# Reordering the ramp of a fused chunk-selecting attention and softplus MLP kernel: weights between the first blocks, later blocks loaded as fp32 and cast on GpSimd, first query tile unselected

## The chip, the cores and the metric

The kernel runs on one core of a Trainium2 chip. The metric is device time in microseconds for one launch; the profile beside it is one profiled execution, read engine by engine (PE is TensorE, DVE is VectorE, ACT is ScalarE, POOL is GpSimd, SP is SyncE, which here only issues DMAs).

## What is computed

```python
# attention: q, k, v are (4, 8, 768, 64) fp32; chunks of 32 keys, the best 6 are kept
k_min, k_max = min/max of k over each chunk
ub = sum(maximum(q * k_min, q * k_max), axis=-1)       # upper bound of a chunk
ub = where(causal, ub, -1e9)
top_chunks = argsort(ub)[..., -6:]
scores = where(selected chunk and key <= query, scale * q @ k.T, -1e9)
attn_out = softmax(scores) @ v
# MLP on x = attn_out as (3072, 512):
h = x @ w_in                                           # w_in (512, 2048)
g = maximum(h, 0) + log1p(exp(-abs(h)))                # softplus
out = g @ w_out                                        # w_out (2048, 512)
```

Among queries 0 to 127 of a batch only four chunks are causal at all, fewer than the six that may be kept.

## The kernel before, in words

The work is cut into 12 blocks (`blocks`, 4 batches of 3) of 256 queries. A block n passes through `loads` or the ramp's loads, `prep`, four `attend` steps (one for each pair of heads), `mlp_h` (64 matmuls of 256 columns on `w_in`, then exp and ln on ACT) and `mlp_y` (32 matmuls of 512 columns on `w_out`).

`prep` transposes k and q, takes each chunk's minimum and maximum (DVE, `kx`), multiplies them with the positive and the negative part of q (PE, L458 and L459), finds the sixth largest with MAX8 (L470), writes a 0/1 row for each chunk into `mr` (L476), transposes `mr` and copies it behind q in the tiles `qab`, so that the score matmul adds the mask by itself. The first three blocks (NRAMP, "the ramp") load fp32 on SP's and ACT's queues into eight buffers `xf` and transpose on PE; the other nine load with a cast to bf16 on POOL's queue (L340, L342) and transpose by DMA (L391, L436, L504, L609).

Every operation is a `Task` with an engine, a duration and a priority. `Graph.schedule` plays the program with these numbers and emits the tasks in the order in which it started them; each engine then runs its own list in that order. `after=` holds a task back in this plan only. On the chip an instruction waits for the buffers and tiles that it touches and, if it issues a DMA, for the DMA eight before it on the same kind of queue, and for nothing else. So a late instruction holds everything behind it on its engine, wherever the plan had put it.

Before the change the plan puts the four `w_in` and `w_out` groups (twelve DMAs on POOL's queue, L311 and L317) behind the attention of the first two blocks and in front of the causal masks of the third, which POOL makes as well (L562, one for each head pair's half). `when_att` and `when_mlp` are the priorities; MSTART is the time at which the MLP's begin.

Of the kernel before, what the change touches and what calls it, by code (L numbers as in the profile page):

```python
# [32 lines left out]
NRAMP = 3  # L33


LAT = {"PE": 0.23, "ACT": 0.20, "DVE": 0.15, "POOL": 0.15, "SP": 0.0}
PSUM_CAP = {"s": 3, "h": 3, "y": 2, "o": 2, "t": 3}
# [7 lines left out]
class Task:  # L45
    __slots__ = ("n", "eng", "dur", "lat", "fn", "prio", "deps", "users", "bufs", "wait",
                 "ready", "start", "end", "dma", "name", "order")


class Graph:  # L50
# [6 lines left out]
    def add(self, eng, dur, fn, prio, r=(), w=(), dma=None, lat=None, name="", after=()):  # L57
        t = Task()
        t.n, t.eng, t.dur, t.fn, t.prio, t.dma, t.name = len(self.tasks), eng, dur, fn, prio, dma, name
        t.lat = LAT[eng] if lat is None else lat  # L60
        deps, bufs = set(after), []
# [22 lines left out]
    def schedule(self):  # L84
# [36 lines left out]
        def flow(to):  # L121
            nonlocal moved
            while moved < to:
                live = [q for q in queues.values() if q]
                if not live:
                    moved = to
                    return
                step = min(min(q[0][0] for q in live) * len(live), to - moved)
                moved += step
                for q in live:  # L130
                    q[0][0] -= step / len(live)
# [8 lines left out]
        while True:  # L140
            nxt = events[0][0] if events else None
            live = [q for q in queues.values() if q]
            if live:
                cand = moved + min(q[0][0] for q in live) * len(live)
# [6 lines left out]
            while events and events[0][0] <= now + 1e-9:  # L151
# [10 lines left out]
                elif what == "queue":  # L162
                    queues.setdefault(x.eng, []).append([x.dma, x])
            for e in LAT:
# [26 lines left out]
                else:  # L191
                    post(now + 1.1, "queue", t)
# [4 lines left out]
def build(nc, tiles):  # L197
# [20 lines left out]
    MSTART = 28.0  # L218
# [3 lines left out]
    ahead = 1.16  # L222
# [43 lines left out]
    for i in range(2):  # L266
# [6 lines left out]
        def oh(which, i):  # L273
            dst = T("ka", i)[64:96] if which == "ka" else T("kb", i)[32:64]
            src = T("ohb").rearrange("c (j s) -> c j s", s=128).unsqueeze(2)
            PO.tensor_copy(dst, src.to_broadcast([32, NQT, NP, 128]))
        for which in ("ka", "kb"):
            add("POOL", 2.7, lambda which=which, i=i: oh(which, i), -6 + i * 34, r=["ohb"], w=[(which + "c", i)],
                name="oh" + which)
# [14 lines left out]
    for n in range(NRAMP):  # L294
        for nm in "kqv":
            for t in range(NT):
                b_ = XF[nm, n, t] = Buf("xf")
                eng = "ACT" if n == 0 and t == 1 else "SP"
                dur = 0.6

                def ld(nm=nm, n=n, t=t, b_=b_, eng=eng):
                    (AC if eng == "ACT" else SP).dma_start(
                        out=T(b_).rearrange("s (h d) -> s h d", h=H), in_=rows(nm, n, t))
                add(eng, dur, ld, -100 + n * 10 + "kqv".index(nm), w=[b_], dma=1.17, lat=0.5, name=f"ld{nm}{n}{t}")

    gate = []


    def ld_win(half, kt):
        fs = slice(half * DFF // 2, (half + 1) * DFF // 2)  # L310
        PO.dma_start(out=T("w_in")[:, kt, fs], in_=moe_w_in()[kt * 128:(kt + 1) * 128, fs])  # L311

    def moe_w_in():
        return srcs["w_in"]

    def ld_wout(c4):
        PO.dma_start(out=T("w_out")[:, c4 * 4:(c4 + 1) * 4, :],  # L317
                     in_=srcs["w_out"][c4 * 512:(c4 + 1) * 512, :].rearrange("(kt ki) f -> ki kt f", ki=128))

    WGATE = []  # L320

    def weights():
        for half in range(2):
            for kt in range(KDM):
                add("POOL", 0.55, lambda half=half, kt=kt: ld_win(half, kt), 14 + half * 2 + kt * 0.1,
                    w=[("w_in", half, kt)], dma=1.38, lat=0.7, name="ldw_in", after=WGATE)
        for c4 in range(4):
            add("POOL", 0.75, lambda c4=c4: ld_wout(c4), 20 + c4, w=[("w_out", c4)], dma=3.1, lat=0.7, name="ldw_out",
                after=WGATE)

    def loads(n):
        base = when_att[n, 0] - 30
        for i, nm in enumerate("kqv"):
# [3 lines left out]
            for t in range(NT):  # L337
                def ld(nm=nm, n=n, t=t, b_=b_):
                    if nm == "v":
                        PO.dma_start(out=v_dst(n, t), in_=rows(nm, n, t))  # L340
                    else:
                        PO.dma_start(out=T(b_)[:, t].rearrange("s (h d) -> s h d", h=H), in_=rows(nm, n, t))  # L342
                b, blk = blocks[n]
                w = [("v", b % 2, blk * NT + t)] if nm == "v" else [(b_, t)]
                add("POOL", 0.9, ld, max(base, 24 + n) + i, w=w, dma=2.1, lat=0.7, name=f"ld{nm}{n}")
# [4 lines left out]
    def prep(n):  # L350
# [9 lines left out]
        ub_sb, mr = Buf("ub"), Buf("mr")  # L360
        if ramp:
            for t in range(NT):
                j = blk * NT + t
                xk = XF["k", n, t]
                kT = ps("t")

                def tr(xk=xk, kT=kT):
                    for p in range(NP):
                        PE.transpose(T(kT)[:, p * 128:(p + 1) * 128], T(xk)[:, p * 128:(p + 1) * 128], T("identf"))
                add("PE", 0.44, tr, pr, r=[xk, "identf"], w=[kT], name=f"kT{n}")  # L370

                def ka(kT=kT, j=j):
                    AC.copy(T("ka", i)[0:64, j], T(kT)[0:64].rearrange("d (p s) -> d p s", p=NP))

                def kb(kT=kT, j=j):
                    AC.copy(T("kb", i)[64:128, j], T(kT)[64:128].rearrange("d (p s) -> d p s", p=NP))

                def red(m, kT=kT, t=t):
# [393 lines left out]
```

## Time and profile before

| | |
|---|---|
| median of 3 runs | 299.5 us (298.94 to 299.71) |
| profiled execution | 298.97 us, of which the span is 297.3 us |
| busy: PE, ACT, DVE, POOL | 252.8, 198.4, 151.6, 113.5 us |
| mean granted clock of TensorE | 0.948 of full speed |

A span is cut by instructions: what an engine waits for is named at the end of its row, and the wait is time before that row's start. Where PE is busy without a gap, only less work for it can shorten the time; where it has gaps, the releaser named is what to follow.

### The profile page before, as it was taken

The numbers are of one execution on the slowest core, as the hardware profiler recorded it, in microseconds if no ns is written. First come the engines' busy times: TensorE is split into PE (matmuls) and PEld (weight loads), VectorE is DVE, ScalarE is ACT, GpSimd is POOL, SyncE is SP. The second block draws the span as 40 slices with busy tenths as digits, with TensorE's granted clock in tenths as the row PEclk, the third lists the DMA queues.
The fourth block names the chain that finished last, engine by engine and source line by source line (L and its number), as shares of the span: only waits on it lengthen the run. The fifth ranks groups of instructions, "written<-read, shape, count | busy, mean of one in ns | idle before, by whom it ended". The sixth has DMA issues, their size and how long they took to land.

```text
span 297.3 us, 6510 instructions
## 1 busy us (share of the span) xinstructions
PE 252.8 (85%) x2465; PEld 188.0 (63%) x2496; DVE 151.6 (51%) x553; ACT 198.4 (67%) x355; POOL 113.5 (38%) x184
## 2 busy tenths in 40 slices
PE   2637652705999999999999999999999999999994
PEld 2416541504896776678766677786867867767661
DVE  5899999631641235376237864175897411010001
ACT  2435760523689674889957398994878968949470
POOL 8956896535591132034654251243312211110000
PEclk9999995565699999999999999999999999999999
DMA  8995999999997158999999984699544211020001
GB/s 162 217 217 113 107 144 153 183 196 173 111 109 72 66 60 125 128 121 90 71 144 173 119 135 54 109 134 113 143 92 56 73 35 72 4 71 37 35 35 71
DMA packets 119647, 32.14 MB, mean 108 GB/s; under 512 B 113472, under 2 KB 115520, under 8 KB 119616
## 3 DMA queue, kind: packets, MB, share of 16 engines
q0 software_dynamic: 59424, 11.28, 47.7%
q1 hardware_dynamic: 57072, 19.67, 35.5%
q10 hardware_dynamic: 3120, 0.79, 1.5%
q8 instruction: 19, 0.31, 0.5%
q14 instruction: 12, 0.10, 0.1%
HBM read 27.26 MB, written 6.29 MB: 113 GB/s over the span
## 4 chain that ended last, share of the span: by engine, by line
PE 69%; DMA 12%; DVE 11%; issue 2%; POOL 2%; ACT 1%; SPq 1%; DVEq 0%; ACTq 0%
PE ps L629 27%; PE ps L651 25%; DMA w_out_sb<-in_moe_w_out_dram 6%; PE ps L542 6%; PE ps L572 6%; DMA w_in_sb<-in_moe_w_in_dram 3%; PE ps L547 3%; DVE kx L379 2%; DMA qab<-kq 2%; PE ps L545 1%; DMA xf<-in_k_dram 1%; DVE ub L470 1%; DVE mr L476 1%; DVE qpn L444 1%; DVE bd L413 1%
## 5 line engine op out<-in xcount | busy, mean ns | idle before, releaser
L556 ACT ACTIVATE pt<-ps 128x512 bf16<-128x512 f32 (+1 forms) x192 | 92.1, 574 | 35.0 <-PE ps L547 26.4
L629 PE MATMUL ps<-x,w_in_sb 128*128 128x256 bf16 x768 | 106.3, 272 | 0.1
L651 PE MATMUL ps<-w_out_sb,g 128*128 128x512 bf16 x353 | 99.2, 379 | 1.2
L629 PEld LDWEIGHTS <-w_in_sb 128*128 128x128 bf16 x768 | 73.2, 98 | 26.9
L636 ACT ACTIVATE e<-ps 128x512 f32<-128x512 f32 x96 | 57.3, 620 | 37.9 <-PE ps L629 37.4
L562 POOL TENSOR_SCALAR_AFFINE_SELECT pt<-pt 128x256 bf16<-128x256 bf16 x96 | 40.1, 427 | 104.5 <-ACT pt L556 103.8
L640 ACT ACTIVATE g<-e 128x1024 bf16<-128x1024 f32 x48 | 51.6, 1076 | 0.9
L656 DVE COPY yo<-ps 128x512 f32<-128x512 f32 x24 | 16.5, 691 | 56.0 <-PE ps L651 55.2
L651 PEld LDWEIGHTS <-g 128*128 128x128 bf16 x384 | 35.5, 98 | 14.9 <-ACT g L640 0.2
L572 PE MATMUL ps<-v,pt 128*128 128x65 bf16 x672 | 31.3, 200 | 10.8 <-POOL pt L562 10.7
L572 PEld LDWEIGHTS <-pt 128*128 128x128 bf16 x672 | 28.5, 102 | 14.7 <-POOL pt L562 11.1
L581 DVE RECIPROCAL st<-ps 128x4 f32<-128x4 f32 x48 | 8.4, 178 | 49.9 <-PE ps L572 37.9
L542 PE MATMUL ps<-qab,ka 96*128 96x256 bf16 x96 | 27.1, 297 | 4.4 <-DVE qab L493 4.3
L542 PE MATMUL ps<-qab,kb 128*128 128x256 bf16 x96 | 26.9, 291 | 0.2
L342 POOL DMA_DIRECT2D kq<-in_k_dram x18 | 16.2, 903 | 20.9 <-DMA kt<-kq 18.1
L395 DVE TENSOR_REDUCE kx<-kt 128x32 bf16<-128x1024 bf16 x18 | 21.1, 1212 | 0.7 <-DMA kt<-kq 0.7
L342 POOL DMA_DIRECT2D kq<-in_q_dram x18 | 16.3, 907 | 12.8 <-DMA qab<-kq 9.3
L340 POOL DMA_DIRECT2D v<-in_v_dram x18 | 16.2, 905 | 6.8 <-DMA w_out_sb<-in_moe_w_out_dram 4.3
L470 DVE MAX8 ub<-ub 128x8 f32<-128x8 f32 (+2 forms) x192 | 16.2, 159 | 0.2
L593 DVE TENSOR_TENSOR oall<-ps,st 128x256 bf16<-128x256 f32 x36 | 15.0, 422 | 0.9
L458 PE MATMUL ps<-bd,qpn 128*128 128x16 bf16 (+2 forms) x96 | 8.2, 181 | 7.2 <-DVE qpn L444 7.2
L542 PEld LDWEIGHTS <-ka 96*128 96x128 bf16 x96 | 10.0, 104 | 6.5 <-issue 2.2
(63 smaller groups left out, 255.5 us busy)
## 6 DMA issues: line engine op xcount, KB each, us to landing
out_dram<-yo SPq DMA_DIRECT2D x24, 256.0 KB, 2.1
kq<-in_k_dram POOLq DMA_DIRECT2D x18, 128.0 KB, 5.8
kq<-in_q_dram POOLq DMA_DIRECT2D x18, 128.0 KB, 4.7
v<-in_v_dram POOLq DMA_DIRECT2D x18, 128.0 KB, 5.1
w_in_sb<-in_moe_w_in_dram POOLq DMA_DIRECT2D x8, 256.0 KB, 8.9
w_out_sb<-in_moe_w_out_dram POOLq DMA_DIRECT2D x4, 512.0 KB, 15.7
xf<-in_k_dram SPq DMA_DIRECT2D x5, 256.0 KB, 7.1
xf<-in_q_dram SPq DMA_DIRECT2D x5, 256.0 KB, 6.0
```

The source lines that it names most:

```text
L342: PO.dma_start(out=T(b_)[:, t].rearrange("s (h d) -> s h d", h=H), in_=rows(nm, n, t))
L395: DV.tensor_reduce(T(kx)[:, m].rearrange("d p (t c) -> d t p c", t=NT), T(kt).rearrange("d (t p) (c s) -> d t p c s", t=NT, s=CH), axis=AX ...
L470: DV.max(out=T(ub_sb)[:, t, e, NCH:NCH + 8], in_=T(ub_sb)[:, t, e, 0:ncc])
L542: PE.matmul(T(sp)[:, 0:QB].rearrange("k (t s) -> k t s", t=NT), kk[r0:r1, j, p], qv[r0:r1, :, p], start=True, stop=True)
L556: AC.activation(T(pt)[:, j:j + 2].rearrange("k j c -> k (j c)")[:, 0:w], T(sp)[:, 0:w], ACT.Exp, scale=SCALE)
L562: PO.affine_select(out=diag, in_=diag, compare_op=ALU.is_ge, fill=0.0, base=0, channel_multiplier=-1, pattern=[[0, 2], [1, 128]])
L572: PE.matmul(o[:, u, h], T(pts[h])[:, j, c0:c0 + 128], T("v", i)[:, j, 2 * p + h, :], start=(j == 0), stop=(j == t0 + u))
L629: PE.matmul(o, T("w_in")[:, dt, ft * 128:(ft + 1) * 128], xv[:, :, dt], start=(dt == 0), stop=(dt == KDM - 1))
L636: AC.activation(T(e)[:, f2 * 2:f2 * 2 + 2].rearrange("f a s -> f (a s)"), T(hp), ACT.Exp)
L640: AC.activation(T(gb)[:, f4 * 4:(f4 + 1) * 4], T(e), ACT.Ln, bias=1.0)
L651: PE.matmul(T(y), T(gb)[:, f, u * 128:(u + 1) * 128], T("w_out")[:, f, :], start=(f == 0), stop=(f == KFF - 1))
L656: add("DVE", 0.6, lambda y=y, yo=yo: DV.tensor_copy(T(yo), T(y)), pr, r=[y], w=[yo], name=f"yo{n}")
```

## The change

The ramp's k and q are loaded as halves by heads (two DMAs a buffer), so that each half of `prep` covers two head pairs and all rows, not four head pairs and half the rows; the tiles `ka`, `kb`, `qab`, `x`, `kq` change their order of axes to match. `w_in` is loaded in four pieces by columns behind block 1's loads in the plan, block 2's loads behind the third of these, `w_out` behind block 2's q, and the later blocks behind the third piece of `w_out`. The later blocks' 54 loads become plain fp32 DMAs on SP into `xf` (at most four buffers in flight) and 54 casts on POOL. The 0/1 rows of keys (`ohb`) are copied in twelve pieces in place of four. In the first block of each batch the first 128 queries have no selection: their mask rows are set to zero by a memset. MSTART goes from 28 to 20.

```diff
+LEAD = 30
+DMA_START = 1.3
+MSTART = 20.0
-            PO.tensor_copy(dst, src.to_broadcast([32, NQT, NP, 128]))
-        for which in ("ka", "kb"):
-            add("POOL", 2.7, lambda which=which, i=i: oh(which, i), -6 + i * 34, r=["ohb"], w=[(which + "c", i)],
+            PO.tensor_copy(dst, T("ohb")[:, ks].unsqueeze(1).to_broadcast([32, NP, QB]))
+        for blk in range(NBLK):
+            for which in ("ka", "kb"):
+                add("POOL", 0.95, lambda which=which, i=i, blk=blk: oh(which, i, blk), -6 + i * 34 + blk * 5, r=["ohb"],
...
+                    else:
+                        for u in range(NT):
+                            q_.dma_start(out=dst[:, u * 4:u * 4 + 4], in_=rows(nm, n, u)[:, t * 4:t * 4 + 4])
...
-        for half in range(2):
-            for kt in range(KDM):
-                add("POOL", 0.55, lambda half=half, kt=kt: ld_win(half, kt), 14 + half * 2 + kt * 0.1,
+    def w_in_load(base, after):
+        for c4 in range(4):
+            def ld(c4=c4):
+                PO.dma_start(out=T("w_in")[:, :, c4 * 512:(c4 + 1) * 512],
+                             in_=srcs["w_in"][:, c4 * 512:(c4 + 1) * 512].rearrange("(kt ki) f -> ki kt f", ki=128))
...
+    def gates(n):
+        return [landed["wi", 2]] if n == 2 else []
+
+    ramp_loads(0, -100)
+    ramp_loads(1, -90)
+    w_in_load(-50, [landed[1, "q", 1]])
+    ramp_loads(2, -80)
+    w_out_load(-40, [landed[2, "q", 1]])
+    LGATE = [landed["wo", 2]]
...
-                        PO.dma_start(out=T(b_)[:, t].rearrange("s (h d) -> s h d", h=H), in_=rows(nm, n, t))
+                    SP.dma_start(out=T(xf).rearrange("s (h d) -> s h d", h=H), in_=rows(nm, n, t))
+                add("SP", 0.6, ld, base + i, w=[xf], dma=1.17, lat=0.6, name=f"ld{nm}{n}", after=LGATE)
+                        PO.tensor_copy(T(b_)[:, :, t], T(xf).rearrange("s (p c) -> s p c", p=NP))
...
+        sel = range(1 if blk == 0 else 0, NT)
...
+        elif blk == 0:
+            add("DVE", 0.15, lambda: DV.memset(T(mr)[:, :, 0, 32:96], 0.0), pr + 0.4,
...
-                    add("PE", 0.438, hm, pr + 0.01 * fi, r=[(x, p) for p in range(NP)] + [("w_in", half, k) for k in range(KDM)],
+                    add("PE", 0.438, hm, pr + 0.01 * fi, r=[(x, p) for p in range(NP)] + [("w_in", f4)],
```

How the change moves instructions, at three places. First POOL before, from block 1's last attention on (`pt` is a causal mask, `kq` and `v` are loads of later blocks):

```order
L562 AFFINE_SELECT pt_111<-pt_111 128x2x128
L513 CAST v_70<-xf_78 128x8x64
L340 DMA v_74<-in_v_dram 128x8x64
L311 DMA w_in_sb<-in_moe_w_in_dram 128x1024 x8
L562 AFFINE_SELECT pt_112<-pt_112 128x2x128
L562 AFFINE_SELECT pt_113<-pt_113 128x2x128
L317 DMA w_out_sb<-in_moe_w_out_dram 128x4x512 x4
L340 DMA v_74<-in_v_dram 128x8x64
L342 DMA kq_86<-in_k_dram 128x8x64 x2
L342 DMA kq_87<-in_q_dram 128x8x64 x2
L562 AFFINE_SELECT pt_114<-pt_114 128x2x128
```

and POOL now, from block 0's first mask on, in two pieces:

```order
L285 COPY kb_76<-ohb 32x4x256
L285 COPY ka_75<-ohb 32x4x256
L285 COPY kb_76<-ohb 32x4x256
L612 AFFINE_SELECT pt_110<-pt_110 128x2x128
L326 DMA w_in_sb<-in_moe_w_in_dram 128x4x512 x4
L612 AFFINE_SELECT pt_111<-pt_111 128x2x128
```

```order
L612 AFFINE_SELECT pt_112<-pt_112 128x2x128
L334 DMA w_out_sb<-in_moe_w_out_dram 128x4x512 x4
L612 AFFINE_SELECT pt_113<-pt_113 128x2x128
L569 CAST v_70<-xf_79 128x8x64
L569 CAST v_70<-xf_78 128x8x64
L612 AFFINE_SELECT pt_114<-pt_114 128x2x128
```

`w_in` now follows the first of block 0's eight masks and `w_out` the mask of block 1's last head pair; between `w_out` and the next mask there is no load any more.

Second SP now, from block 1's v on (`xf_83` and so on are the eight fp32 buffers):

```order
L316 DMA xf_80<-in_v_dram 128x8x64
L319 DMA xf_83<-in_k_dram 128x4x64 x2
L319 DMA xf_82<-in_k_dram 128x4x64 x2
L319 DMA xf_84<-in_q_dram 128x4x64 x2
L319 DMA xf_85<-in_q_dram 128x4x64 x2
L316 DMA xf_79<-in_v_dram 128x8x64
L316 DMA xf_78<-in_v_dram 128x8x64
L360 DMA xf_81<-in_k_dram 128x8x64
L360 DMA xf_80<-in_k_dram 128x8x64
L360 DMA xf_83<-in_q_dram 128x8x64
L360 DMA xf_82<-in_q_dram 128x8x64
L360 DMA xf_84<-in_v_dram 128x8x64
```

Block 2's loads (L319, L316) follow block 1's directly and block 3's (L360) follow those; no instruction between them stands for the plan's `after`.

Third DVE before, in block 0's selection (`ub` are the bounds; `x2` at a row's end counts equal neighbours):

```order
L379 TENSOR_REDUCE kx_102<-ps_139 128x4x4 x2
L267 MEMSET bd_77 128x192
L413 COPY bd_73<-kx_102 64x8x8 x2
L444 TENSOR_SCALAR qpn_98<-qab_92 128x512
L446 TENSOR_SCALAR qpn_99<-qab_92 128x512
L444 TENSOR_SCALAR qpn_98<-qab_92 128x512
L446 TENSOR_SCALAR qpn_99<-qab_92 128x512
L448 COPY qab_93<-qab_92 64x512 x2
L464 TENSOR_TENSOR ub_104<-ps_142,cmask 128x8x8
L269 MEMSET v_74 128x48
L464 TENSOR_TENSOR ub_104<-ps_142,cmask 128x8x8
L470 MAX ub_104<-ub_104 128x8 x16
```

and DVE now at the same place (L280 is a memset of block 3's key tile):

```order
L405 TENSOR_REDUCE kx_102<-ps_139 128x16 x2
L278 MEMSET v_74 128x48
L280 MEMSET kb_76 32x1536
L440 COPY bd_73<-kx_102 64x8x8 x2
L477 TENSOR_SCALAR qpn_98<-qab_93 128x2x128
L479 TENSOR_SCALAR qpn_99<-qab_93 128x2x128
L477 TENSOR_SCALAR qpn_98<-qab_93 128x2x128
L479 TENSOR_SCALAR qpn_99<-qab_93 128x2x128
L481 COPY qab_92<-qab_93 64x512 x2
L505 TENSOR_TENSOR ub_104<-ps_142,cmask 128x4x8 x2
L532 MEMSET qab_93 32x4x64
L514 MAX ub_104<-ub_104 128x8 x8
```

There are 8 MAX rows where before there were 16, and the memset of `kb_76`, which before came after block 0's selection, stands in front of it.

## Rows read from the trace of the kernel before

**Rows 1.** Windows: busy us of each engine, instructions, granted clock, DMA share, GB/s.
```profile
0.00:42.60 42.60, 23.67 (x242) 18.54 (x242) 37.47 (x128) 21.67 (x42) 34.59 (x49) 1.00 1.22 161
42.60:80.00 37.40, 17.48 (x192) 13.75 (x189) 20.82 (x85) 12.00 (x26) 21.19 (x33) 0.59 1.47 169
80.00:290.00 210.00, 208.20 (x2026) 154.32 (x2054) 91.94 (x341) 164.69 (x288) 57.76 (x103) 1.00 0.69 88
```

**Rows 2.** Timeline of PE: start, us, instruction, idle before it and releaser.
```profile
62.79 0.46 PE L572 MATMUL ps<-v,pt 128*128 128x65 bf16 x5 [3.62 <-POOL pt L562]
69.49 0.90 PE L572 MATMUL ps<-v,pt 128*128 128x65 bf16 x13 [6.25 <-POOL pt L562]
...
79.95 1.48 PE L629 MATMUL ps<-x,w_in_sb 128*128 128x256 bf16 x12
```

**Rows 3.** Timeline of POOL.
```profile
28.01 1.17 POOL L513 CAST v<-xf 128x512 bf16<-128x512 f32 x2
...
41.87 4.33 POOL L311 DMA_DIRECT2D w_in_sb<-in_moe_w_in_dram  x8
...
61.43 0.87 POOL L342 DMA_DIRECT2D kq<-in_q_dram  x1 [2.92 <-DMA w_out_sb<-in_moe_w_out_dram]
```

**Rows 4.** Chain that ended last, two of its pieces: start, us, what.
```profile
43.52 8.50 DMA w_in_sb<-in_moe_w_in_dram
...
52.30 18.67 DMA w_out_sb<-in_moe_w_out_dram
```

**Rows 5.** Timeline of PE near the end, matmuls back to back.
```profile
267.66 4.09 PE L629 MATMUL ps<-x,w_in_sb 128*128 128x256 bf16 x36
...
287.22 6.21 PE L651 MATMUL ps<-w_out_sb,g 128*128 128x512 bf16 x28
```

**Rows 6.** Timeline of PE, first score matmuls of block 0 and of block 1.
```profile
22.62 0.37 PE L542 MATMUL ps<-qab,ka 96*128 96x256 bf16 x1 [1.83 <-DVE qab L493]
...
33.35 0.27 PE L542 MATMUL ps<-qab,ka 96*128 96x256 bf16 x1 [1.55 <-DVE qab L493]
```

**Rows 7.** Timeline of DVE.
```profile
13.90 1.11 DVE L470 MAX8 ub<-ub 128x8 f32<-128x8 f32 x16
14.93 1.46 DVE L476 TENSOR_TENSOR mr<-ub 128x64 bf16<-128x64 f32 x1
...
16.39 2.78 DVE L476 TENSOR_TENSOR mr<-ub 128x64 bf16<-128x64 f32 x1
...
25.22 1.34 DVE L271 MEMSET kb<- 32x1536 uint32 x1 [0.27 <-issue]
...
35.31 0.28 DVE L606 COPY x<-ps 128x256 bf16<-128x256 bf16 x1
...
50.88 0.21 DVE L476 TENSOR_TENSOR mr<-ub 128x64 bf16<-128x64 f32 x1
```

**Rows 8.** Timeline of POOL beside it.
```profile
13.58 2.74 POOL L276 COPY ka<-ohb 32x3072 bf16<-32x3072 bf16 x1
16.36 2.74 POOL L276 COPY kb<-ohb 32x3072 bf16<-32x3072 bf16 x1
```

**Rows 9.** Timeline of ACT.
```profile
9.12 1.07 ACT L430 CAST qab<-ps 128x512 bf16<-128x512 f32 x2
...
55.42 5.56 ACT L556 ACTIVATE pt<-ps 128x512 bf16<-128x512 f32 x12 [12.32 <-PE ps L547]
...
269.80 1.06 ACT L640 ACTIVATE g<-e 128x1024 bf16<-128x1024 f32 x1
270.76 1.63 ACT L636 ACTIVATE e<-ps 128x512 f32<-128x512 f32 x3
```

**Rows 10.** Windows, as rows 1.
```profile
8.00:22.00 14.00, 6.28 (x43) 4.54 (x41) 13.41 (x40) 5.06 (x9) 10.95 (x7) 1.00 1.45 217
60.00:70.00 10.00, 0.96 (x15) 0.81 (x16) 2.30 (x6) 0.98 (x3) 3.73 (x5) 0.59 1.23 196
```

**Rows 11.** DMA issues: queue, operation, count, median us to landing.
```profile
kt<-kq SPq DMA_TRANSPOSE x9, 4.5
```

More of the change, by code (lines that the diff above doesn't have):

```diff
@@ L46 @@
     __slots__ = ("n", "eng", "dur", "lat", "fn", "prio", "deps", "users", "bufs", "wait",
-                 "ready", "start", "end", "dma", "name", "order")
+                 "ready", "start", "end", "dma", "name", "order", "pkt")
 class Graph:
@@ L55, in __init__, with add @@
         self.pools, self.caps = pools, caps
[L57 removed]
+    def add(self, eng, dur, fn, prio, r=(), w=(), dma=None, lat=None, name="", after=(), pkt=18):
         t = Task()
@@ L293, in build, with ramp_loads @@
     XF, KQ = {}, {}
-    for n in range(NRAMP):
+    landed = {}
+    def ramp_loads(n, base):
         for nm in "kqv":
-            for t in range(NT):
+            for t in range(2):
                 b_ = XF[nm, n, t] = Buf("xf")
                 eng = "ACT" if n == 0 and t == 1 else "SP"
[L299 to L322, printed above, removed]
-        for half in range(2):
-            for kt in range(KDM):
-                add("POOL", 0.55, lambda half=half, kt=kt: ld_win(half, kt), 14 + half * 2 + kt * 0.1,
-                    w=[("w_in", half, kt)], dma=1.38, lat=0.7, name="ldw_in", after=WGATE)
-        for c4 in range(4):
-            add("POOL", 0.75, lambda c4=c4: ld_wout(c4), 20 + c4, w=[("w_out", c4)], dma=3.1, lat=0.7, name="ldw_out",
-                after=WGATE)
+                def ld(nm=nm, t=t, b_=b_, eng=eng):
+                    dst = T(b_).rearrange("s (h d) -> s h d", d=D)
+                    q_ = AC if eng == "ACT" else SP
+                    if nm == "v":
+                        q_.dma_start(out=dst, in_=rows(nm, n, t))
+                    else:
+                        for u in range(NT):
+                            q_.dma_start(out=dst[:, u * 4:u * 4 + 4], in_=rows(nm, n, u)[:, t * 4:t * 4 + 4])
@@ new lines, in tr, with kab @@
+                    xv = T(xk).rearrange("s (t p c) -> s t p c", t=NT, p=2)
+                    for p in range(2):
+                        for t in range(NT):
+                            c0 = (p * NT + t) * 128
+                            PE.transpose(T(kT)[:, c0:c0 + 128], xv[:, t, p], T("identf"))
+                add("PE", 0.44, tr, pr + 0.01 * hh, r=[xk, "identf"], w=[kT], name=f"kT{n}")
+                def kab(which, rs, kT=kT, p2=p2):
+                    AC.copy(T(which, i)[rs, p2, ks_], T(kT)[rs].rearrange("d (p s) -> d p s", p=2))
@@ L386, in prep @@
+                add("ACT", 0.48, lambda kab=kab: kab("kb", slice(64, 128)), pr + 0.2, r=[kT],
+                    w=[("kb", i, j, hh) for j in js], name=f"kb{n}")
         else:
@@ L665, in build @@
         prep(n)
-    weights()
     for n in range(NRAMP):
```

305 lines of the change are left out of this document (168 added, 137 removed).

## The prediction

> **What bounds the kernel now.** I read the windows first. They show three stages [rows 1]. From 80 to 290 us PE is busy 208.20 of 210.00 us at a granted clock of 1.00: there the kernel is bound by PE, and nothing but less PE work shortens it. Up to 42.60 PE has 23.67 us of work and DVE is busy for 37.47 us: the ramp goes at DVE's pace. Between 42.60 and 80 no engine is full, and the granted clock is 0.59, near the lower of TensorE's two levels (1.2 GHz).
>
> The timeline of PE tells why. In that middle stage PE waits 3.62 and 6.25 us for a causal mask of POOL, and the first matmul of the MLP starts at 79.95 [rows 2]. POOL is late because its list holds twelve weight loads and loads of later blocks, each of which waits for the DMA eight before it: it issues `w_in` at 41.87, and at 61.43 a load of q still waits 2.92 us for `w_out` [rows 3]. The chain of waits runs through the same place, with 8.50 us in `w_in` and 18.67 us in `w_out` [rows 4].
>
> So I count by lost time: the time of a point less the PE work in front of it at full rate. 36 matmuls of 256 columns take 4.09 us and 28 of 512 take 6.21 [rows 5]; less the tail of the last one this is 0.109 and 0.216 us each. With these and, as estimates by columns or by the smallest spacing in the trace, 0.055 for 128 columns, 0.031 for a 65 column one, 0.026 for a bound and 0.11 for an fp32 transpose, the whole kernel is 236.5 us of PE, of which 24.2 stand in front of the first MLP matmul (48 fp32 transposes, 80 bounds, 46 other transposes, 102 score and 152 value matmuls). It starts at 79.95, so 55.8 us are lost by then. Behind it 212.3 us of work take until 293.4, where the last matmul ends [rows 5]: 1.2 us lost in 213.5. The last copy and store take 3.9 to the span's end (297.3), and 1.7 lie around the span (298.97, 0.5 below the median of 299.5). In a formula, time = lost + PE work + 1.2 + 3.9 + 1.7; for before 55.8 + 236.5 + 6.8 = 299.1. What the change does to the 55.8 us is the question.
>
> **The change, part by part.**
>
> *Unselected first tile.* 32 of 192 bound matmuls (0.8 us) and four mask transposes (0.2) go: PE work 235.5. On DVE block 0 loses 8 of 16 MAX8 (1.11 us for 16 [rows 7], so 0.55), and about 0.7 us of half-width operations, by the same halving.
>
> *Key rows in smaller copies.* Before, the comparison L476 takes 1.46 and 2.78 us in block 0 and 0.21 in a later one [rows 7], and its two ends (16.39 and 19.17) lie just behind those of POOL's copies (16.32 and 19.10) [rows 8]: DVE stands still until POOL's 2.74 us copy is over. A third of a copy is 0.91 us, so of the 3.8 us lost between 0.5 and 1 remain. The Trainium skill has this as a rule (SBUF — State Buffer, "Who interferes with whom"): a DVE instruction with two SBUF inputs and a GpSimd instruction that reads SBUF exclude each other for a whole instruction. The trace agrees: by that rule the first two comparisons lose 3.8 us here, as measured. The same rule speaks against the 54 new casts, each of which could hold DVE for its whole length.
>
> *The memset moved forward.* L280 stands now in front of block 0's selection and costs its 1.34 us there [rows 7]; it is gone from behind it. These parts give 0.5 + 0.7 + 3.0 − 1.3 = 2.9 us. A further 1.3, an estimate, comes from the order of halves: the first score needs the masks of two head pairs only, so two of block 1's reductions and half of the mask copies go behind it. Block 0's scores then start at about 18.4, not 22.62 [rows 6]. Block 1's scores wait for DVE too (33.35 [rows 6]). Between the two DVE gets back the 1.3 us that was put off and loses the 1.34 of the memset, so nearly all of the gain stays: 3.9 us, 29.5. Block 0's x, complete at 35.6 [rows 7], is then complete at about 31.5.
>
> *Where the weights land.* The plan's `after` holds nothing on the chip. Block 2's loads follow block 1's as buffers come free, and `w_in` waits on POOL only for block 0's first mask, some 1.3 us behind its first score: 19.7. The price of a piece of weights (1 MB read, 0.52 MB written): in the stretch 60 to 70, nearly all `w_out`, 196 GB/s [rows 10] make 2.7 us; all twelve weight loads, seven others among them, took from 41.87 to 70.97 [rows 3, 4], so at most 3.6 for each of eight. With 2 us to start and five fp32 loads of 0.262 MB in between at 217 GB/s [rows 10], 1.2 us each, the first piece lands between 25 and 28 and the last between 36 and 43. The MLP takes the first piece at 31.5 and the last at about 43. I take 2.7, since that stretch is most like the new one: `w_in` is hidden. `w_out` follows block 1's last mask but one, at about 38.5; its pieces land at 44 to 52, up to 61 at the higher price, and are wanted from 47.5 to 55.
>
> *From block 1 to block 2.* Between block 1's first score and block 2's first score PE has 13.7 us of work, 56 MLP matmuls in it. ACT has 16 exponentials of attention (12 such in 5.56 us [rows 9], so 0.46 each, a little less with the shorter half: 6.9), 7 of the MLP at 0.51 (3.6), 2 logarithms at 0.96 (1.9) (both from the starts in [rows 9]) and 6 copies of 0.55 to 0.6 (two take 1.07 [rows 9]; 3.6 with the gap behind them): 16.0. ACT is the longer. Block 2's scores then start at 29.5 + 0.4 + 16.0 = 45.9, with 20.9 us of PE work in front: 25.0 lost. DVE's part of block 2 lies beside it: between the first scores of blocks 0 and 1, where DVE prepares one block and finishes another, 10.7 us pass [rows 6]. In the next stretch, to block 1's first MLP matmul, ACT has 10.4 us and PE 9.7: 25.7 lost. Behind it PE is the longer again (11.6 to 10.7).
>
> *Later blocks.* Each gives POOL six casts of 0.58 us (two took 1.17 [rows 3]) for six DMA issues, and SP six more issues. Block 3's chain is the tightest: casts behind block 2's masks at 56, transposes of 4.5 us to landing [rows 11], some 9 us of DVE behind them (the 10.7 less the attention in it), mask transposes, taken as 4.5 too, scores ready at about 76; PE comes there at 53 + 25.7 = 79. 3 us are over, and for later blocks more. So I cost this part at nothing; what hides it is PE's own MLP work in front of each block.
>
> *Sum.* 25.7 lost. For waits of an in-order list that rows of before cannot show (a `w_out` piece, a PSUM buffer) I add 2, between 0 and the 6 by which the last `w_out` piece would be late at the higher price. Lost 27.7 + 235.5 + 6.8 = 270.0 us. That is 29.5 us below the median, 28 of it lost time and 1 PE work.
>
> **The rivals.**
>
> *Weights and loads crowd each other, or TensorE's clock stays low.* For it: `w_in` shares the DMA engines with fp32 loads in small packets, and the clock was 0.59 where PE had 17.48 us of work in 37.40 [rows 1]. At the higher price `w_out` costs 6 us: 276. At the lower clock the 13.7 us of PE work before block 2's scores become 27.4 where ACT gives 16.0, 11.4 more: 281. Against: PE would be busy for 85% of that stretch, and in the first 42.60 us before, busy for 56%, the clock was granted in full [rows 1].
>
> *ACT doesn't bind and all is hidden.* If PE runs without a gap from 29.5 on, with 7.2 us of work in front, 22.3 are lost: 264.6. Against: the 16.0 us of ACT.
>
> *Later blocks starve PE (the side of slower).* Load, cast, two kinds of transposes and masks of one block hang on SP's and POOL's lists in turn, and one late cast holds every load and transpose behind it on SP. The price is what a block is late beyond its margin of about 3 us. To lose the whole gain each of nine blocks must be 3.3 us late beyond it: 300 and more, and slower from there. For it: 54 casts, 31 us in all, may each stop DVE. Against: DVE is busy for 92 of 210 us in the steady stage [rows 1], and POOL's work gets less.
>
> *The change moves nothing.* If the middle stage is bound by bytes and not by POOL's list, the weights still take 29.1 us from the first issue to the last landing (41.87 to 70.97 [rows 3, 4]). From 19.7 this ends at 48.8 if `w_out` follows at once, and at 57 to 61 if it waits for its mask: the time is 270 to 276, the forecast's upper part. Only weights issued no earlier than before would give 299.5, and the order on POOL speaks against it.
>
> **How the numbers follow.** Forecast, 264 to 276: 0.62. Crowding or clock, 276 to 285: 0.20. All hidden, below 264.6: 0.08. Starved in part, 285 to 298: 0.05. Slower than 300.4: 0.03; within 0.3% (about what a measurement of this kernel can tell from no change): 0.02. The predicted time is 270.0. The range 262 to 282 leaves out starvation and the far end of crowding, and on the low side takes in a ramp 2 us shorter than I can argue. Faster 0.95, same 0.02, slower 0.03.
>
> **What the new profile would show.** Right: block 0's scores near 18.4, block 1's near 29.5, the first `w_in` matmul near 31.5 and not waiting for a DMA; block 2's scores near 46 behind ACT; PE busy for 99% from about 57 on; L522 below 0.9 us each. Wrong: PE waiting for `w_in` or `w_out`; a granted clock well below 1 between 30 and 57; gaps of PE in front of scores of later blocks that end with a DMA transpose or a cast.

## The result and the profile after

The changed kernel takes 282.13 us (median of 4, 280.93 to 283.38), the kernel before 299.22: a ratio of 0.943 [0.938, 0.948]. The sign was right. The time is 12.1 us above the forecast of 270.0 and just outside its range of 262 to 282. One run, with other places for the weights, came to 275.16. Times and ratios here and below leave out four executions in a slower state (one of e3, one of e8, two of e9).

The profiled execution took 280.93 us (span 279.2), 1.2 below the median. In windows the stages look so (busy us of each engine, granted clock, DMA share, GB/s; the share adds up the times of all packets and can exceed 1); [rows 1] are those of before:

```profile
20.00:30.00 10.00, 6.77 (x61) 5.16 (x59) 7.66 (x36) 4.88 (x11) 8.84 (x16) 0.86 0.96 155
30.00:40.00 10.00, 8.91 (x87) 7.28 (x88) 5.73 (x24) 5.66 (x13) 2.45 (x6) 0.63 1.08 187
40.00:50.00 10.00, 7.09 (x84) 5.66 (x83) 7.50 (x26) 7.83 (x15) 5.43 (x9) 1.00 0.87 152
50.00:60.00 10.00, 9.89 (x113) 7.89 (x114) 5.53 (x29) 9.40 (x19) 1.22 (x3) 1.00 1.04 168
...
80.00:100.00 20.00, 18.78 (x207) 14.13 (x208) 19.24 (x77) 15.18 (x29) 10.76 (x22) 1.00 1.04 218
...
160.00:180.00 20.00, 17.21 (x165) 12.45 (x166) 11.10 (x39) 12.90 (x23) 4.89 (x10) 1.00 0.61 144
...
60.00:260.00 200.00, 192.66 (x1953) 143.43 (x1984) 107.60 (x401) 155.95 (x279) 64.63 (x131) 1.00 0.71 138
```

The stage of 37 us in which PE had 17.48 us of work is gone. What is left are a stretch at a low clock between 20 and 40, and 7.34 us of PE's idle time from 60 to 260, where the steady stage of before lost 1.8 in 210 [rows 1]. Some 1.7 to 1.8 us of each of these is no wait: the profile holds 348 of the 384 matmuls on `w_out` (353 before), and a missing one shows as a gap of some 0.05 us.

The timeline of PE in the ramp answers to [rows 2] and [rows 6]:

```profile
18.60 0.80 PE L597 MATMUL ps<-qab,ka 96*128 96x256 bf16 x4 [0.56 <-DVE qab L551]
...
32.46 0.91 PE L597 MATMUL ps<-qab,ka 96*128 96x256 bf16 x4 [0.41 <-DVE qab L551]
...
35.40 1.06 PE L679 MATMUL ps<-x,w_in_sb 128*128 128x256 bf16 x4
...
39.91 0.61 PE L398 MATMUL ps<-identf,xf 128*128 128x128 f32 x4
...
49.39 0.18 PE L498 MATMUL ps<-bd,qpn 128*128 128x48 bf16 x1 [0.89 <-DVE ub L505]
...
52.42 0.60 PE L597 MATMUL ps<-qab,ka 96*128 96x256 bf16 x4
```

Block 0's scores start at 18.60 (forecast 18.4), block 1's at 32.46 (29.5), the first `w_in` matmul at 35.40 without a wait for its DMA (31.5), block 2's scores at 52.42 (45.9). The row to look at is 39.91: block 2's k is transposed only there. SP and POOL show that this k had been asked for long before, and when the weights were:

```profile
13.48 3.01 SPq L319 DMA_DIRECT2D xf<-in_k_dram  x4
```
```profile
20.26 3.11 POOL L326 DMA_DIRECT2D w_in_sb<-in_moe_w_in_dram  x4
```

Those loads of k are issued from 13.48 to 16.49. The ten loads of this kind land a median of 4.2 us after their issue, so k lies there from about 21, an estimate. The transposes wait for nothing; they stand behind the first MLP matmuls on PE's list. The plan keeps block 2's loads behind `w_in`'s third piece, and the chip, which has no such gate, follows the order that the plan wrote.

### The profile page after: what moved, and what is told of

It is laid out like the page before. It is cut to its first block, busy times and chain, and to the rows that moved or that the text cites. A ratio compares the mean times of both kernels' runs of the same rounds, so it can differ in the third digit from the quotient of the medians.

```text
span 279.2 us, 6479 instructions
## 1 busy us (share of the span) xinstructions
PE 248.9 (89%) x2424; PEld 184.4 (66%) x2460; DVE 152.5 (55%) x558; ACT 198.6 (71%) x355; POOL 98.3 (35%) x188
## 2 busy tenths in 40 slices
DMA packets 120800, 39.23 MB, mean 140 GB/s; under 512 B 113600, under 2 KB 117696, under 8 KB 120768
## 3 DMA queue, kind: packets, MB, share of 16 engines
q1 hardware_dynamic: 113392, 33.83, 62.7%
## 4 chain that ended last, share of the span: by engine, by line
PE 62%; DVE 16%; DMA 13%; ACT 4%; issue 3%; SPq 1%; POOL 0%; DVEq 0%; ACTq 0%
PE ps L679 22%; PE ps L700 21%; PE ps L597 10%; DMA kt<-kq 6%; PE ps L622 5%; DMA xf<-in_q_dram 4%; DVE kx L423 3%; DVE kx L405 2%; DMA qab<-kq 2%; ACT pt L606 2%; DVE qpn L479 1%; DMA xf<-in_k_dram 1%; ACT kb L402 1%; DVE qpn L477 1%; DVE oall L643 1%
## 5 line engine op out<-in xcount | busy, mean ns | idle before, releaser
L606 ACT ACTIVATE pt<-ps 128x512 bf16<-128x512 f32 (+1 forms) x192 | 93.1, 568 | 16.8 <-PE ps L597 14.7
L705 DVE COPY yo<-ps 128x512 f32<-128x512 f32 x24 | 16.4, 685 | 45.7 <-PE ps L700 45.7
L367 POOL CAST kq<-xf 128x512 bf16<-128x512 f32 x36 | 22.5, 627 | 35.2 <-DMA xf<-in_k_dram 22.4
L597 PE MATMUL ps<-qab,kb 128*128 128x256 bf16 x192 | 32.9, 269 | 0.2
L597 PE MATMUL ps<-qab,ka 96*128 96x256 bf16 x192 | 30.1, 269 | 1.8 <-DVE qab L551 1.0
L622 PE MATMUL ps<-v,pt 128*128 128x65 bf16 x672 | 29.8, 196 | 2.0 <-POOL pt L612 1.9
L597 PEld LDWEIGHTS <-ka 96*128 96x128 bf16 x192 | 18.4, 101 | 10.6 <-issue 2.4
L597 PEld LDWEIGHTS <-kb 128*128 128x128 bf16 x192 | 17.6, 102 | 6.7 <-DVE qab L551 0.2
L514 DVE MAX8 ub<-ub 128x8 f32<-128x24 f32 (+2 forms) x160 | 14.1, 160 | 0.1
L498 PE MATMUL ps<-bd,qpn 128*128 128x32 bf16 (+2 forms) x80 | 7.2, 179 | 7.7 <-DVE qpn L477 4.7
L365 POOL CAST v<-xf 128x512 bf16<-128x512 f32 x18 | 11.1, 621 | 6.8 <-DMA xf<-in_v_dram 6.7
## 6 DMA issues: line engine op xcount, KB each, us to landing
w_out_sb<-in_moe_w_out_dram POOLq DMA_DIRECT2D x4, 512.0 KB, 11.1
```

The costliest lines, as they stand in the source:

```text
L367: PO.tensor_copy(T(b_)[:, :, t], T(xf).rearrange("s (p c) -> s p c", p=NP))
L597: PE.matmul(T(sp)[:, z * QB:z * QB + QB - q0], kk[r0:r1, p, (j + z) * 128:(j + z + 1) * 128], qq[r0:r1, p, q0:QB], start=True, stop=True)
L606: AC.activation(T(pt)[:, j:j + 2].rearrange("k j c -> k (j c)")[:, 0:w], T(sp)[:, 0:w], ACT.Exp, scale=SCALE)
L622: PE.matmul(o[:, u, h], T(pts[h])[:, j, c0:c0 + 128], T("v", i)[:, j, 2 * p + h, :], start=(j == 0), stop=(j == t0 + u))
L705: add("DVE", 0.6, lambda y=y, yo=yo: DV.tensor_copy(T(yo), T(y)), pr, r=[y], w=[yo], name=f"yo{n}")
```

## The experiments

Two numbers describe each run: the lost time at block 2's first score (its start less the PE work in front of it, at the prediction's prices), and PE's idle time from 60 to 260 us. In the last column both are taken from the span of the same profile. It stays within 239 to 244, so the two numbers explain a run to within some 5 us and no better. The profiled execution can be the fastest of its kernel (the changed one) or the slowest (e11), so that differences of a few us are read from the times.

```
kernel                            us     ratio to before [95%]  block 2's score  work   lost  idle   rest
changed                         282.13  0.943 [0.938, 0.948]        52.42        20.9   31.5   7.3   240.4
e1  weights behind block 2      275.16  0.918 [0.912, 0.923]        44.70        17.7   27.0   4.7   241.5
e2  loads cut to one head       276.34  0.922 [0.917, 0.927]        53.44        20.9   32.5   3.3   239.0
e3  casts cut to one head       282.44  0.939 [0.933, 0.946]        52.44        20.9   31.5   9.8   240.6
e4  weights early, old loads    298.83  0.998 [0.995, 1.001]          -            -      -   18.8     -
e5  e1, AHEAD 1.08              275.30  0.922 [0.917, 0.927]        44.89        17.7   27.2   5.1   240.8
e6  new loads, weights as before 281.02 0.940 [0.935, 0.946]        47.11        15.9   31.2   6.1   241.1
e7  e1, key rows later          279.31  0.934 [0.930, 0.939]        46.79        18.1   28.7   7.3   242.1
e8  e7, AHEAD 1.08              277.49  0.928 [0.922, 0.934]        44.85        18.1   26.8   6.7   241.3
e9  changed, all selected       282.05  0.946 [0.938, 0.953]        52.95        22.1   30.8   7.3   243.9
e10 e1 and e2                   274.26  0.919 [0.914, 0.923]        44.37        17.7   26.7   3.6   242.3
e11 e1, w_in issued early       277.97  0.929 [0.924, 0.934]        47.37        17.7   29.7   6.6   241.6
e12 changed, w_in issued late   284.23  0.949 [0.945, 0.953]        54.80        20.9   33.9   7.6   241.7
```

The idle times of e9 and e10 can't be set beside the others as they stand: their profiles hold all 384 matmuls on `w_out`. Without the gaps under 0.1 us the idle time is 5.5 us in the changed kernel, 2.6 in e1, 1.4 in e2, 7.7 in e3, 7.1 in e9 and 3.4 in e10.

**Weights planned behind block 2's loads (e1).**

```diff
-        return [landed["wi", 2]] if n == 2 else []
+        return []
-    w_in_load(-50, [landed[1, "q", 1]])
     ramp_loads(2, -80)
-    w_out_load(-40, [landed[2, "q", 1]])
+    w_in_load(-50, [landed[2, "q", 1]])
+    w_out_load(-40, [landed["wi", 3]])
```

> The changed kernel, but in the plan w_in comes behind block 2's loads and holds nothing back (block 2's loads were never held on the chip). Theory (plan order): in the changed kernel block 2's k waits from about 20 us to 39.9 us for its place in PE's list, since the plan believes it to land behind w_in; with the preparation placed early, block 2's scores start at 46 to 48 us and not at 52.4, and the time falls by 3 to 5 us, to about 278. Rival (the weights between the blocks are needed there): w_in is issued some 4 us later, the first MLP matmul waits for it, and the time stays or rises by 0 to 4 us, 282 to 286.

The timeline of PE:

```profile
25.69 0.63 PE L398 MATMUL ps<-identf,xf 128*128 128x128 f32 x4
...
33.79 0.54 PE L597 MATMUL ps<-qab,ka 96*128 96x256 bf16 x4 [1.55 <-DVE qab L551]
...
36.32 1.03 PE L679 MATMUL ps<-x,w_in_sb 128*128 128x256 bf16 x4
...
44.70 0.77 PE L597 MATMUL ps<-qab,ka 96*128 96x256 bf16 x6
```

Block 2's k is transposed 14 us earlier. Block 0's and block 1's scores and the first `w_in` matmul come about 1 us *later* than in the changed kernel, and yet 7.0 us are gained, more than the 3 to 5 expected: block 2's scores come 7.7 earlier, with 3.2 us less work in front, so 4.5 us less are lost there, and the idle time behind falls by 2.6. (The 1 us in front is chance: e10, with the same lists, starts block 0's scores at 18.59, and e12, with those of the changed kernel, at 19.59.) `w_in`, issued at 28.65, still keeps no matmul waiting; one weight load of PE waits 0.59 us for it.

**The same two orders with `w_in`'s place exchanged (e11, e12).** PE's list is in each pair the same; only the four issues stand elsewhere on POOL's list, which is rewritten after the plan is made:

```diff
     order = graph.schedule()
+    wi = [t for t in order if t.name == "ldw_in"]
+    order = [t for t in order if t.name != "ldw_in"]
+    at = next(i for i, t in enumerate(order) if t.name == "cm0") + 1              # e11
+    at = max(i for i, t in enumerate(order) if t.name == "ohkb") + 1              # e12
+    order[at:at] = wi
```

> The order of the first run (weights planned behind block 2's loads, 275.2 us), but with the four issues of w_in put back behind block 0's first mask on GpSimd's list, where the changed kernel has them. All other lists stay as in the first run: block 2's k transposes stand behind 5.9 us of PE's work, not behind 12.3. Theory (the place of block 2's transposes on PE's list makes the difference of 7 us): w_in is issued near 20 and the time is 274 to 276.5. Rival (w_in issued at 20 crowds block 2's loads on the DMA engines, and that delays block 2): block 2's first scores at 48 or later and 279 or more.

> The other corner: the changed kernel (282.1 us) with the four issues of w_in moved back on GpSimd's list, behind the last of the key-row copies, and all other lists as they were. Theory (PE's list): w_in is issued at 30 or a little later, the first w_in matmul waits for it at first by up to 4 us, and nothing is gained: 281.5 to 285. Rival (crowding by the early issue): the time falls to 278 or less.

e12 came as the theory said, with its first `w_in` matmul 1.14 us late at its DMA. e11 fell between its theory and its rival: 4.2 us below the changed kernel and 2.8 above e1, each known to about 2 us by the intervals. Its POOL and its PE:

```profile
21.23 3.10 POOL L326 DMA_DIRECT2D w_in_sb<-in_moe_w_in_dram  x4
```
```profile
24.82 0.33 PE L622 MATMUL ps<-v,pt 128*128 128x65 bf16 x5 [0.57 <-POOL pt L612]
...
26.74 0.61 PE L622 MATMUL ps<-v,pt 128*128 128x65 bf16 x6 [0.55 <-POOL pt L612]
...
27.77 1.09 PE L398 MATMUL ps<-identf,xf 128*128 128x128 f32 x4
```

POOL is in `w_in`'s issues until 24.33, block 0's masks stand behind them, PE's value matmuls wait for the masks, and block 2's transposes behind those move from 25.69 to 27.77. Nothing in these rows waits for a transfer. The granted clock is lower too, in e1 first and then in e11:

```profile
30.00:40.00 10.00, 7.04 (x80) 5.26 (x81) 9.82 (x47) 5.91 (x14) 4.93 (x10) 0.83 1.12 184
```
```profile
30.00:40.00 10.00, 7.28 (x56) 5.68 (x55) 9.82 (x46) 5.61 (x12) 2.54 (x5) 0.67 1.22 208
```

Between 20 and 50 us e11 loses 5.1 us of full-rate time to the clock (0.88, 0.67 and 0.94 in steps of 10 us) and e1 1.7. So POOL's time and the clock together cost the 2.8 us, and how much each was not separated. The changed kernel loses the same 5.1 us to the clock as e11 does. So of the 7.0 us between the changed kernel and e1, 4.2 belong to the order of the lists, at an equal loss to the clock, and 2.8 to the place of the issues, with what follows from it.

**The parts of the change by themselves (e4, e6, e9).** e4 is the kernel before with the weight loads of the changed one, its MSTART of 20 and its plan gate on the later blocks' loads, which stay on POOL. e6 is the changed kernel with its weights issued where the kernel before has them; with that go MSTART back to 28 and both plan gates (on block 2's loads and on the later ones). e9 selects the first tile again. The lines that matter:

```diff
+    w_in_load(-50, [landed[1, "q", 1]])                                # e4, in the kernel before
+    w_out_load(-40, [landed[2, "q", 1]])
...
-        return [landed["wi", 2]] if n == 2 else []                     # e6, in the changed kernel
+        return []
-    w_in_load(-50, [landed[1, "q", 1]])
-    w_out_load(-40, [landed[2, "q", 1]])
+    held = [t for t in g.tasks if t.name == "vc2"]
+    w_in_load(14, held)
+    w_out_load(20, held)
...
-        sel = range(1 if blk == 0 else 0, NT)                          # e9, in the changed kernel
+        sel = range(0, NT)
...
```

> The kernel before with the order of the weights alone: w_in by columns behind block 1's loads in the plan, w_out behind block 2's, the priorities' start at 20, and the later blocks still loaded with a cast on POOL's queue; all of the first tile selected, key rows in long copies. Theory (POOL's list with the weights in it was the bound): most of the gain comes, block 2's scores at 55 to 58 us, 285 to 288 us. Rival (the cast loads on POOL are as much to blame): masks wait behind loads that wait for the DMA eight before them, and the time is 292 to 299.

> The other corner to the fourth run: later blocks' fp32 loads by the hardware queue and the first tile unselected, as in the changed kernel, but w_in and w_out issued where the kernel before has them, behind block 2's v casts, and the MLP's start in the planned order put back to 28. The fourth run had the weights' order alone and gained nothing (298.8 us), so either the loads are the whole gain or the two complement each other. Theory (they complement: a shorter ramp is worth only what later loads can follow): the ramp is as before, with the first h at 40 or later, later blocks no longer starve, and the time lies between, 284 to 292. Rival (the loads are the whole gain): 282 or less. Rival (the loads gain nothing by themselves either): 296 to 300.

> The changed kernel with the first query tile of each first block selected as the others are, as the kernel before did. The prediction gave the unselected tile 1.0 us of PE's work and a quarter to a half of a first block's selection on VectorE. Theory: block 0's scores come 1 to 2 us later (19.6 to 20.6 for 18.6), PE's work grows by about 1 us, and the time is 283 to 285. Rival (block 0's preparation is off the path that sets the end, since the ramp behind it waits for block 2's k and the granted clock): within 1 us of the changed kernel's 282.1. Second rival: as in the two runs in which block 0 came earlier and the time did not fall, an order that packs the front less tightly ends earlier, below 281.

e4 missed its expectation and came to its rival's time. The weights are issued at 17.23 and PE is full from 40 to 50, but then the later blocks starve. Its windows, its POOL and its PE:

```profile
40.00:50.00 10.00, 10.00 (x147) 8.74 (x145) 7.24 (x40) 8.89 (x19) 2.84 (x7) 0.90 0.81 131
...
140.00:160.00 20.00, 9.88 (x117) 6.46 (x116) 12.93 (x45) 7.10 (x15) 12.65 (x16) 0.78 1.23 86
```
```profile
90.91 0.88 POOL L341 DMA_DIRECT2D kq<-in_k_dram  x1 [7.57 <-DMA kt<-kq]
...
91.79 1.68 POOL L559 TENSOR_SCALAR_AFFINE_SELECT pt<-pt 128x256 bf16<-128x256 bf16 x4
```
```profile
92.28 0.68 PE L569 MATMUL ps<-v,pt 128*128 128x65 bf16 x6 [2.09 <-POOL pt L559]
...
159.24 4.00 PE L626 MATMUL ps<-x,w_in_sb 128*128 128x256 bf16 x18 [10.01 <-DMA x<-oall]
```

A load on POOL that waits 7.57 us for a buffer holds up the masks behind it, and PE waits 2.09 us for these. The largest wait is another: 10.01 of the 18.8 us idle are one wait for the DMA transpose of a block's x, issued on SP at 150.06 and landing 9.1 us later, while POOL issues ten loads between 147.68 and 156.58. That these loads delay it was not tested. From 140 to 160 PE has 9.88 us of work in 20. What the ramp gains is lost again: 298.83.

e6 gives 281.02, which is the changed kernel's time and its rival's forecast. The gain of the change thus comes without the weights' new place, from the new loads together with the small edits of the front; the new loads alone were not run. But e6 is two steps away from the changed kernel. It frees block 2's transposes, which stand at 24.52 in it, and its first `w_in` matmul comes at 42.29, 6.9 us later. So weights between blocks 1 and 2, with the gate that they put on block 2's loads, gain nothing over the old place without that gate. e1, with the weights planned behind block 2's loads and no gate on these, shows what was to be had (275.16).

e9 is undecided: block 0's scores come at 20.38, which is 0.8 to 1.8 later than the two starts that the changed kernel's lists show, block 1's at 32.60, only 0.14 later, and the intervals of the two kernels overlap.

**What the later blocks lose (e2, e3, e5, e10).** e2 loads one head of eight of each later block, e3 casts one head or pair of heads from the seventh block on, e5 lets attention run ahead of the MLP by less, e10 is e1 with e2's edit. In e2, e3 and e10 the rest of those inputs is left out.

```diff
-                    SP.dma_start(out=T(xf).rearrange("s (h d) -> s h d", h=H), in_=rows(nm, n, t))      # e2, e10
+                    SP.dma_start(out=T(xf).rearrange("s (h d) -> s h d", h=H)[:, 0:1], in_=rows(nm, n, t)[:, 0:1])
+                    if n >= 6:                                                                          # e3
+                        if nm == "v":
+                            PO.tensor_copy(v_dst(n, t)[:, 0:1], T(xf).rearrange("s (h d) -> s h d", h=H)[:, 0:1])
+                        else:
+                            PO.tensor_copy(T(b_)[:, 0, t], T(xf)[:, 0:128])
...
-AHEAD = 1.16                                                                                            # e5, in e1
+AHEAD = 1.08
```

> The changed kernel with the later blocks' 54 loads cut to one of eight heads (the rest of the buffers keeps what it held, so this part of the input is left out); every wait and cast stays. Theory (DMA pace): from 60 to 260 us PE is idle for 7.35 us in the changed kernel because the DMA engines need about as long for a block as PE gives them; with an eighth of the bytes this falls to about 2 us and the time by 5 us, to 277. Rival (casts on POOL hold DVE): the casts are all there, so the idle time stays above 6 us and the time within 1 us of 282.

> The changed kernel with the casts of the blocks from the seventh on cut to one of eight heads (q and k: one of four pairs), so that the rest of these blocks' input is left out; every load stays whole. Theory (DMA pace): the time stays within 1 us of 282 and PE's idle time from 60 to 260 us stays at 6 us or more. Rival (casts hold DVE): PE's idle time falls by 3 us or more and the time to 278 or 279.

> Both weights issued behind block 2's loads as in the first experiment (275.2 us), and the factor AHEAD by which attention runs ahead of the MLP in PE's order lowered from 1.16 to 1.08, so that a block's scores are asked for later and the MLP's matmuls are spread more evenly beside them. Theory (the DMA engines set the pace between 60 and 170 us, since more blocks are asked for per microsecond there than they bring): PE's idle time from 60 to 260 us falls from about 4.5 us to 2 or less, the ramp stays as it is, and the time is 271 to 273. Rival (the gaps there are hand-offs between engines that belong to each block, wherever it stands): the same number of gaps, only spread, and 274.5 to 276. Second rival: less MLP is left to fill other gaps, or more of it stands at the end without cover: above 276.

> Weights issued behind block 2's loads (275.2 us), and with it the later blocks' loads cut to one head of eight, the rest of those tiles being left unread from memory: what is computed is not the reference's. Theory (ramp and DMA pace are two separate losses): the ramp is that of the first run, with block 2's scores near 44.7, PE's idle time from 60 to 260 us falls from 4.7 to 2 or less, and the time is 271.5 to 273. Rival (the loads matter only where the ramp is long): 274.5 to 276.

The chain of waits of the changed kernel shows the mechanism (start, us, what):

```profile
151.97 5.88 DMA kt<-kq
...
160.90 4.62 DMA xf<-in_q_dram
165.51 5.65 DMA kt<-kq
171.19 2.35 DVE kx L423 x2
```

A load of q, the transpose of the same block's k, which stands behind the loads on SP's list, and the reduction follow each other with PE waiting at the end (1.30 us at 174.01). With the loads cut PE's idle time falls from 7.3 to 3.3 us and the time to 276.34, with a ramp that is no shorter, and the transposes of k land a median of 3.1 us after their issue in place of 4.7. With the casts of the blocks from the seventh on cut, POOL has 12.2 us less work from 60 to 260 and PE's idle time does not fall. The theory holds, but for this order only. In e1 the cut gains nothing: gaps of 0.1 us and more make 2.6 us without it and 3.4 with it, and the ratio stays (0.918 and 0.919). The 274.26 lie just under the rival's 274.5 to 276. There VectorE is what is full; windows of e10:

```profile
80.00:100.00 20.00, 19.05 (x202) 13.55 (x200) 18.25 (x76) 14.95 (x29) 10.25 (x22) 1.00 0.59 120
...
120.00:140.00 20.00, 18.77 (x242) 14.91 (x241) 19.66 (x80) 17.47 (x37) 12.96 (x25) 1.00 0.68 119
```

PE's gaps stand where DVE has 18.25 and 19.66 us of work in 20. That DVE binds there was not tested. AHEAD (e5) moved gaps from one window to the next and gained nothing, as its rival had it.

**The key rows of the second buffer later (e7, e8).**

```diff
+        if i == 0:
+            keys(0, [])          # DVE's memset and the key-row copies of buffer 0, as before
...
+    keys(1, [t for t in g.tasks if t.name == "mb1"])
```

With the copies of the second buffer goes DVE's memset of it (L280, 1.34 us).

> Weights behind block 2's loads as in the first experiment, and the six GpSimd copies of the one-hot key rows of the second buffer (1.03 us each) with VectorE's memset of that buffer moved behind block 1's masks, out of the first 18 us. Theory (the stalls that VectorE takes beside GpSimd's copies delay block 0's preparation): block 0's first scores fall from 19.6 to 17 to 18, block 1's follow by as much, and the time is 272.5 to 274. Rival (the hand-offs between VectorE and ScalarE on one PSUM bank bind there): block 0's scores within 0.5 us of 19.6 and 275 to 276. Second rival: the copies, now later, hold up block 1's keys, and block 1's scores come later than 33.8: above 276.

> The two edits before this one together: the key rows later and AHEAD 1.08. If they work on different stretches (ramp and 60 to 170 us) their gains add, to 269 to 271. If the first is nothing, it equals the run with AHEAD 1.08 alone, and if a shorter ramp only moves the DMA engines' full stretch forward, the sum falls short of both by 1 us or more.

The front answers, and more than expected: block 0's scores start at 16.27 (e1 19.57), block 1's at 31.54 (33.79). And e7 is 4.2 us slower than e1, above all that was expected of it but its second rival, whose reason (later scores of block 1) does not hold. Block 2's scores come at 46.79 (e1 44.70), and the granted clock is 0.51 from 30 to 40, where e1 has 0.83:

```profile
30.00:40.00 10.00, 7.70 (x63) 5.78 (x63) 9.53 (x29) 5.36 (x11) 4.68 (x8) 0.51 1.22 196
```

In e8, with nearly the same ramp, it is 0.66 there and 0.83 before, and block 2's scores come at 44.85. From 20 to 50 both lose 5.1 us of full-rate time to the clock, so the clock's sum is not what sets them apart; between e7 and e1 (1.7) clock and order were not separated. e8 misses the 269 to 271 at which the two edits' gains would add.

## Why the prediction was right in sign and 12 us off

The formula puts the profiled 280.93 at 235.5 of PE work, 5.6 around it, and 39.8 lost; the prediction had 28.9. 6.5 of the difference arise in front of block 2's first scores (3.0 up to block 1's, 3.5 from there), 4.4 behind them.

**Unselected tile, key rows, memset: right in sum, wrong in mechanism.** 18.60 for 18.4. L522 is down to 0.45 us at most. But the stall moved instead of shrinking: in the timeline of DVE a cast and a `tensor_scalar`, with one SBUF input each, end just behind POOL's copies.

```profile
13.67 1.06 DVE L479 TENSOR_SCALAR qpn<-qab 128x256 bf16<-128x256 bf16 x1
...
28.36 1.01 DVE L525 CAST mr<-ub 128x4 bf16<-128x4 f32 x1
```
```profile
13.60 1.04 POOL L285 COPY kb<-ohb 32x1024 bf16<-32x1024 bf16 x1
...
28.23 1.11 POOL L285 COPY ka<-ohb 32x1024 bf16<-32x1024 bf16 x1
```

Of the same two shapes a `tensor_scalar` takes 0.21 just before it (L477 at 13.54) and a cast 0.16. The prediction took only the rule for two SBUF inputs; the same section of the Trainium skill (SBUF — State Buffer, "Who interferes with whom") says that copies, casts and `tensor_scalar` can contend with GpSimd for the shared ports too, when their operands meet the conditions of a two-port mode. These rows agree with it. In e7 block 0's scores come 2.3 to 3.3 us earlier (16.27 for 18.59 or 19.57); the memset of 1.34 us that moved with the copies is part of that, so 1.0 to 2.0 are left for the stalls, an estimate.

**Where the weights land: right, and worth nothing as it was done.** `w_in` is issued at 20.26 (19.7) and nobody waits for it. But the step took for granted that earlier is better. e6 and e11 show that it isn't always: the old place, with block 2 freed of the gate, does as well, and the issues' 3.1 us on POOL push block 0's masks back.

**From block 0 to block 1: 3.0 us late.** Between the two first scores 13.86 us pass, not 11.1. DVE has 11.28 us of work in them (10.24 before) and waits 2.2 us for ACT and PE (not at all before), which the forecast, with DVE alone, did not have. In e12, where `w_in`'s issues don't stand in front of block 0's masks, it is 12.89, so about 1.0 goes with these issues. The rest was not separated.

**From block 1 to block 2: the step that failed.** Between the two first scores 19.96 us pass, not 16.4. ACT has 15.52 us of work, as forecast (16.0), but does not bind. In this stretch PE is busy for 17.05 with its 13.7 us of work, at a granted clock of 0.88, and idle for 2.9, all of it between 43 and 50 behind DVE's part of block 2's preparation (the last such wait is the row at 49.39). The prediction set that preparation beside ACT's work, at no cost, without asking where PE's list has its transposes: behind 12.3 us of PE work, as against 5.9 in e1 and e11. In e11, with `w_in` issued behind the same mask and the same 5.1 us lost to the clock from 20 to 50, PE has no idle time left in this stretch, and the kernel is 4.2 us faster. The windows of the changed kernel and of e11 between the two scores:

```profile
32.46:52.42 19.96, 17.05 (x188) 13.96 (x188) 13.22 (x53) 15.52 (x30) 7.47 (x14) 0.88 0.97 168
```
```profile
35.58:47.37 11.79, 11.78 (x145) 9.65 (x145) 10.96 (x51) 10.04 (x20) 5.62 (x12) 0.76 0.87 174
```

The rival "the clock stays low" (276 to 281) was right on the clock (0.63 from 30 to 40) and not on the DMA: no PE instruction waits for weights. The prediction argued against it that PE would be busy for 85% of the stretch. It was, 17.05 of 19.96, but the clock was low before the stretch began (0.86 from 20 to 30).

**Later blocks: costed at nothing, 4.4 us more than the forecast's allowances.** The margin of 3 us took 4.5 us for a transpose and no queue for the loads; in the chain above transposes take up to 5.88 us and a load of q 4.62. The rival had named the casts, and e3 speaks against that for the blocks that it cuts; e2 shows that the loads' bytes and packets matter. The DMA engines are busy for nine tenths in nearly every slice of the profile page up to 160 us, with 113600 of 120800 packets under 512 B. That alone would not show it: in the kernel before they are as busy in most slices up to 180 us, and PE has no wait from 80 on. The Trainium skill (DMA: Bandwidth & Descriptors, "Why small descriptors are slow (HBM only)") puts a fixed cost on each packet; no run here separates it from the bytes. What the profile shows is that hardware queue q1 holds 113392 packets and 62.7% of 16 engines' span of 279.2 us, 25 ns for a packet of 298 bytes on average.

```profile
DMA  8999979949999999999999993412312211040101
...
DMA packets 120800, 39.23 MB, mean 140 GB/s; under 512 B 113600, under 2 KB 117696, under 8 KB 120768
...
q1 hardware_dynamic: 113392, 33.83, 62.7%
```

## What to carry to other kernels

Where a planner writes in-order lists, a gate that exists in the plan alone still decides: ask for each moved transfer what its planned landing does to the place of its consumers on every list, and read that place before costing anything by engine sums. Moving waits off a list that also carries short, urgent work (masks on POOL) was worth some 18 us here, the small edits of the front included (e6), and putting 3 us of issues in front of such work cost 2.8, the lower clock included (e11). A gain at the front of a pipeline need not reach its end: e4 filled PE from 40 to 50 us and e7 shortened the front, and both lost it again.

## What was not expected of the hardware

POOL's copies of a third of the size took 1.03 us, not a third of 2.74, and hold single-input DVE instructions as they held comparisons. The granted clock fell between 20 and 50 us in all thirteen kernels, but not by the same amount: by rows, 1.7 us of full-rate time in e1 (0.83 from 30 to 40) and e5, 3.4 in e10, 5.1 in the changed kernel (0.86 and 0.63) and seven others, 6.8 in e12, 8.5 in e4 (0.75, 0.50, 0.90). In the first 20 us PE was busy for 7.2 us in e1, 8.2 in the changed kernel, 10.2 in e7 (5.1 lost), so a fuller front did not go with a shorter fall. What decides it stays open.
